# Linear attention with RMS norm and a two-layer MLP: the first pair's v through SyncE and a cast, another order of loads, and stage two rearranged

## The chip, the cores and the metric

The kernel runs on one core of one Trainium2 chip. The core has TensorE (PE; its weight loads are shown apart as PEld), VectorE (DVE), ScalarE (ACT), GpSimd (POOL) and SyncE (SP), and 16 DMA engines, which all queues share. SP, ACT and POOL can issue transfers; in this kernel nearly all loads are issued by POOL, and they turn fp32 in DRAM into fp16 in SBUF on the way. The metric is the device time of one execution in microseconds; lower is better.

## The reference, cut to what matters

There are 8 batches, 8 heads, 576 tokens and a head dimension of 64. The tokens of all batches together (4608) are the rows of an MLP from 512 through 2048 to 512.

```python
kv  = einsum('bhsd,bhse->bhde', k, v)          # 64 x 64 for each head
out = einsum('bhsd,bhde->bhse', q, kv)
rms = sqrt(mean(out * out, axis=-1) + 1e-6)
x   = (out / rms * g_norm), heads side by side: 4608 x 512
h   = x @ w_in                                  # 4608 x 2048
g   = max(h, 0) + alpha * min(h, 0)
y   = g @ w_out                                 # 4608 x 512
```

## The kernel before

The order of the work on every engine is written out by hand (`manual_schedule`), so each engine executes its instructions in the order in which the program emits them, and waits only for data and for free buffers.

**Tiling.** The MLP is done in nine windows `w` of 512 tokens. For a window, `x` is held transposed (`xts[w]`, 128 features by four chunks by 512 tokens). The first product makes 16 groups `u` (or `g`) of 128 hidden features each, four matmuls of 512 columns a group (L600, or L945 and L631 where a group is done by columns). ACT takes the negative part (L609) and DVE combines it into `gt` (L615). In window 0 the second product is plain, one matmul for each of 4 row tiles and 16 groups (`y_run(a, (g,))`, L643, 64 in all). In the other windows it is done with seven products of half size, in the manner of Strassen and Winograd, from sums of `w_out` (`w_sum`) and sums of `gt` (`s_sum`); its matmuls are L796. They are spread over the 16 units of the loop by lists: `X_AT` and `YZ_AT` hold how many matmuls of each sort go into a unit, `S_ALL` and its sisters into which unit a sum goes.

**Attention.** Heads are worked in four pairs `j`. `step_kv` makes k-transposed times v for a pair (L403 for batch 0, L418 for batch 1), `mask_kv` copies it to SBUF on DVE; `step_t` transposes q on PE (L336) and copies it; `step_ot` multiplies the two (L437) and squares the result on ACT; `ssq_mm` sums the squares (L460) and takes the inverse root on ACT; `norm` writes `x` (L476 or L474). From window 2 on, the same is done by rows: `row_kv` (L1122), `rows_mm` (L499), `rows_sq`, `rows_rs`, `rows_norm`, and SP transposes by DMA, both q on its way to `qt_sb` (`dma_t`, L380) and `x` on its way to `xts` (L585). `ROW_AT[w]` says in which unit of window `w-1` each of these stands.

**The start.** The heads of pair 0 arrive by themselves: q by SP and k by ACT in fp32 (`early_pair`, L97), and `cast0` turns them into fp16 (q on DVE, k on ACT). v of pairs 0 and 1 comes by POOL in one cast transfer (`load0("v", 0, 2)`, L168). Then POOL issues everything else in the order of the lines from 261 on: q, k, v of the other pairs, the identity matrix between them, six pieces of `w_in` (piece 0 in two halves of its four chunks, piece 0 to 3 for two groups each, 4 and 5 for four groups each), eight pieces of `w_out` (two groups each), and batch 1. While the pairs are worked, `keep_warm` puts matmuls on constant data into PE's idle time. The first four groups of window 0 are begun chunk by chunk as `norm` delivers the pairs (`m1_parts(g, c)` for groups 0 and 1).

**Stage two.** After the 16 groups of window 0, a written list (L990 to L1093) mixes the 64 `y_run` matmuls with the attention of window 1 (`step_t(1, j)`, `step_kv(1, j)`, `step_ot`, `ssq_mm`, `norm`), the scaling of `w_in` by `g_norm` (`scale_w_in`) and the sums of `w_out` (`w_sum`). The three last matmuls of row tile 3 go into the loop.

**The loop's loads.** `LOADS` places the loads of batch `w+2` into units of window `w`. A load placed at unit `at > 1` stands behind a `gate`, a one-element copy on POOL that reads `gt` of unit `at - 1`; POOL's queue stands still until that is there. q of batch 3 and later is loaded in four pieces of 128 tokens and a remainder of 64 (`load_q`, `load_rem`).

Of the kernel before, what the change touches and what calls it, by code (L numbers as in the profile page):

```python
# [9 lines left out]
FP32 = mybir.dt.float32  # L10
# [7 lines left out]
def kernel(  # L18
# [83 lines left out]
    early_pair(nc.sync, "q", "wsum2")  # L102
    early_pair(nc.scalar, "k", "wsum4")
# [119 lines left out]
    def load_w_in(i):  # L223
        f0, f1 = IN_CUTS[i], IN_CUTS[i + 1]
        t = w_p.tile([P, NC, f1 - f0], FP16, name=f"w_in_sb{i}")
        src = moe_w_in[:, f0:f1].rearrange("(c p) f -> p c f", p=P)
        for c in range(0, NC, NC // 2 if i == 0 else NC):
            n = NC // 2 if i == 0 else NC
            nc.gpsimd.dma_start(out=t[:, c : c + n, :], in_=src[:, c : c + n, :])
        w_in_sb.append(t)  # L230
# [707 lines left out]
    keep_warm(1)  # L938
    norm(0, 1)
    step_kv(0, 3)  # L940
# [9 lines left out]
    first = [ps_h.tile([P, W], FP32, name="h_ps", tag="h1")]  # L950
    first += [ps_o.tile([P, W], FP32, name="h_ps", tag="o") for g in range(2)]
    ssq_mm(0, 2, h_at(0))
    for g in range(2):
        m1_parts(g, 0)
# [34 lines left out]

    y_run(0, (0,))  # L990
    y_run(2, (0,))
# [23 lines left out]
    y_run(0, (4,))  # L1015
    y_run(1, (4,))
    y_run(2, (4,))
    scale_w_in(4, 3, 4, nc.scalar)
    scale_w_in(4, 1, 4, nc.scalar)
    scale_w_in(1)  # L1020
    scale_w_in(3)
    y_run(3, (6,))
    scale_w_in(2)
    y_run(2, (5,))
    step_t(1, 2, S_POOL)
    y_run(1, (7,))
# [3 lines left out]
    y_run(2, (7,))  # L1030
    y_run(3, (5,))
    step_kv(1, 0, O_POOL)
    for nm in ("k", "q"):
        nc.vector.memset(bufs[0][nm][REM:P, TPP, :, :], 0.0)
    y_run(0, (7,))
    step_kv(1, 1, S_POOL)
    y_run(1, (5,))
    y_run(3, (7,))
# [4 lines left out]
    ssq_mm(1, 0, S_POOL)  # L1043
    y_run(0, (8,))
    y_run(1, (8,))
    y_run(3, (8,))
    ssq_mm(1, 1, Q_POOL)
    y_run(0, (6,))
    y_run(0, (9,))
    norm(1, 0)  # L1050
    y_run(3, (9,))
# [3 lines left out]
    w_sum(2, 0)  # L1055
    w_sum(3, 1)
    y_run(2, (8,))
    y_run(2, (9,))
    y_run(2, (11,))
    y_run(1, (11,))  # L1060
    y_run(1, (9,))
    ssq_mm(1, 2)
    y_run(2, (10,))
    y_run(2, (13,))
    y_run(1, (10,))
    w_sum(4, 0)
    step_ot(1, 3)
    y_run(0, (11,))
    y_run(0, (12,))
    y_run(0, (10,))  # L1070
    y_run(0, (13,))
    norm(1, 2)
    w_sum(2, 1)
    y_run(2, (12,))
# [3 lines left out]
    norm(1, 3)  # L1078
    y_run(1, (12,))
# [3 lines left out]
    y_run(2, (14,))  # L1083
    y_out(ys[2], 0, 2)
    y_run(0, (15,))
    y_run(1, (15,))
# [4 lines left out]
    step_t_rem(1, Q_POOL)  # L1091
# [23 lines left out]
    def row_kv(bs):  # L1115
# [26 lines left out]
        5, 6, 8, 9), 'rs': (5, 5, 9, 12), 'norm': (5, 6, 9, 12), 'red': (0, 0, 0, 1)}}  # L1142
# [166 lines left out]
```

## Time and profile before

| | us |
|---|---|
| median of 3 runs | 275.2 |
| lowest and highest run | 273.97, 275.27 |
| profiled execution, its own time | 273.96 |
| its span, first to last instruction | 272.1 |
| PE busy | 264.8 |
| DVE busy | 217.1 |
| ACT busy | 156.5 |
| POOL busy | 86.7 |

The times of all transfers and instructions below are on the span's clock. A line of the timeline gives start, duration, engine, source line, operation, tiles, shapes and count, and in brackets how long the engine was idle before it and what ended that. Ends of matmuls are modelled, and matmuls overlap: a matmul of 512 columns is shown with 379 ns, but the next one starts 216 ns after it, so work on PE is counted here by the distance of starts. A line of the chain gives start, length and what it was; the chain is followed back from the last instruction.

### The profile page before, as it was taken

The numbers are of one execution on the slowest core, as the hardware profiler recorded it, in microseconds if no ns is written. First come the engines' busy times: TensorE is split into PE (matmuls) and PEld (weight loads), VectorE is DVE, ScalarE is ACT, GpSimd is POOL, SyncE is SP. The second block draws the span as 40 slices with busy tenths as digits, with TensorE's granted clock in tenths as the row PEclk, the third lists the DMA queues.
The fourth block names the chain that finished last, engine by engine and source line by source line (L and its number), as shares of the span: only waits on it lengthen the run. The fifth ranks groups of instructions, "written<-read, shape, count | busy, mean of one in ns | idle before, by whom it ended". The sixth has DMA issues, their size and how long they took to land.

```text
span 272.1 us, 6163 instructions
## 1 busy us (share of the span) xinstructions
PE 264.8 (97%) x2286; PEld 168.6 (62%) x2286; DVE 217.1 (80%) x413; ACT 156.5 (58%) x532; POOL 86.7 (32%) x130
## 2 busy tenths in 40 slices
PE   7799999999999999999999999999999999999995
PEld 2354444456766676667666666666667666666684
DVE  7359657999958986998699869986998889878963
ACT  3468575785578447754776467546855864433410
POOL 8773462506431644164415431430110011101100
PEclk9999999999999999999999999999999999999999
DMA  7999999998999999969996999693051122211123
GB/s 149 194 201 203 195 198 193 183 212 95 163 159 197 149 166 125 182 110 172 142 149 117 162 142 149 130 168 77 19 137 40 41 55 81 59 39 40 40 77 119
DMA packets 91570, 35.58 MB, mean 131 GB/s; under 512 B 62980, under 2 KB 89748, under 8 KB 91540
## 3 DMA queue, kind: packets, MB, share of 16 engines
q0 software_dynamic: 57872, 23.83, 71.9%
q1 hardware_dynamic: 32628, 10.34, 23.9%
q10 hardware_dynamic: 1040, 1.02, 1.2%
q8 instruction: 18, 0.29, 0.4%
q14 instruction: 12, 0.10, 0.2%
HBM read 36.71 MB, written 9.44 MB: 170 GB/s over the span
## 4 chain that ended last, share of the span: by engine, by line
PE 83%; DMA 13%; POOL 1%; issue 1%; SPq 1%; ACT 0%; DVE 0%; POOLq 0%
PE h_ps L600 38%; PE yY L796 14%; PE yX L796 10%; PE yZ L796 10%; DMA w_out_sb<-in_moe_w_out_dram 5%; PE y L643 4%; DMA w_in_sb<-in_moe_w_in_dram 3%; DMA qst<-in_q_dram 3%; PE h_ps L631 2%; DMA qt_sb<-qst 2%; PE kv_ps L1122 2%; PE or_ps L499 1%; PE yZ L791 1%; SPq L380 1%; PE kv_ps L418 0%
## 5 line engine op out<-in xcount | busy, mean ns | idle before, releaser
L600 PE MATMUL h_ps<-xt,w_in_sb 128*128 128x512 f16 x540 | 136.2, 379 | 0.0
L609 ACT ACTIVATE m_sb<-h_ps 128x512 f32<-128x512 f32 x144 | 86.5, 601 | 80.3 <-PE h_ps L600 61.5
L615 DVE SCALAR_TENSOR_TENSOR gt<-m_sb,beta_sb,h_ps 128x512 f16<-128x512 f32 x144 | 106.2, 743 | 22.0 <-ACT m_sb L609 18.8
L600 PEld LDWEIGHTS <-w_in_sb 128*128 128x128 f16 x540 | 51.4, 98 | 39.4 <-issue 0.2
L655 POOL DMA_DIRECT2D out_dram<-y_sb x32 | 20.5, 644 | 122.0 <-DVE y_sb L838 57.5
L796 PEld LDWEIGHTS <-s 128*128 128x128 f16 x496 | 48.3, 98 | 11.3 <-DVE s L733 0.3
L796 PEld LDWEIGHTS <-gt 128*128 128x128 f16 x384 | 37.5, 98 | 23.2 <-issue 0.2
L796 PE MATMUL yX<-w_out_sb,gt 128*128 128x256 f16 x256 | 44.6, 273 | 0.0
L796 PE MATMUL yY<-wsum,s 128*128 128x256 f16 x256 | 35.2, 273 | 0.0
L562 ACT ACTIVATE sq_sb<-or_ps 128x64 f16<-128x64 f32 x144 | 30.5, 250 | 2.6 <-PE or_ps L499 2.6
L562 ACT ACTIVATION_READ_ACCUMULATOR sq_sb<-or_ps 128x1 f32 x144 | 30.0, 236 | 0.0
L580 DVE TENSOR_TENSOR x_rows<-or_ps,rstd_r 128x512 f16<-128x512 f32 x27 | 18.4, 686 | 1.0 <-ACT rstd_r L572 1.0
L828 DVE TENSOR_TENSOR u<-yY,p 128x512 f32<-128x512 f32 x16 | 11.0, 689 | 9.6 <-PE yY L796 9.6
L185 POOL DMA_DIRECT2D qst<-in_q_dram x20 | 17.7, 904 | 0.1
L796 PE MATMUL yY<-wsum,gt 128*128 128x256 f16 x128 | 17.6, 273 | 0.0
L796 PE MATMUL yZ<-wsum,s 128*128 128x256 f16 x120 | 17.5, 273 | 0.0
L796 PE MATMUL yZ<-w_out_sb,s 128*128 128x256 f16 x120 | 16.7, 273 | 0.0
L643 PE MATMUL y<-w_out_sb,gt 128*128 128x512 f16 x64 | 16.3, 379 | 0.1
L731 DVE TENSOR_TENSOR s<-gt 128x512 f16<-128x512 f16 x32 | 13.3, 419 | 0.1
L733 DVE TENSOR_TENSOR s<-s,gt 128x512 f16<-128x512 f16 x32 | 12.8, 420 | 0.4
L737 DVE TENSOR_TENSOR s<-gt,s 128x512 f16<-128x512 f16 x32 | 12.7, 418 | 0.0
L735 DVE TENSOR_TENSOR s<-gt 128x512 f16<-128x512 f16 x32 | 12.4, 419 | 0.0
(107 smaller groups left out, 231.1 us busy)
## 6 DMA issues: line engine op xcount, KB each, us to landing
out_dram<-y_sb POOLq DMA_DIRECT2D x16, 256.0 KB, 2.8
kst<-in_k_dram POOLq DMA_DIRECT2D x7, 512.0 KB, 9.9
vst<-in_v_dram POOLq DMA_DIRECT2D x6, 512.0 KB, 8.1
qst<-in_q_dram POOLq DMA_DIRECT2D x20, 128.0 KB, 4.6
w_out_sb<-in_moe_w_out_dram POOLq DMA_DIRECT2D x8, 256.0 KB, 11.0
out_dram<-y_sb SPq DMA_DIRECT2D x5, 256.0 KB, 2.2
w_in_sb<-in_moe_w_in_dram POOLq DMA_DIRECT2D x2, 512.0 KB, 10.0
qst<-in_q_dram POOLq DMA_DIRECT2D x2, 512.0 KB, 12.0
```

The costliest lines, as they stand in the source:

```text
L185: nc.gpsimd.dma_start(out=st[:, t, :, :], in_=srcs["q"][b, :, t * P : (t + 1) * P, :].rearrange("h p d -> p h d"),)
L562: nc.scalar.activation(out=sq[:, half, j], in_=o_ps[:, half, j], func=AF.Square, accum_out=ssq[:, half, j : j + 1],)
L580: nc.vector.tensor_tensor(out=xr[:].rearrange("p j h d -> p h j d"), in0=o_ps, in1=rstd[:].unsqueeze(3).to_broadcast([P, 2, NPAIR, D]), op ...
L600: nc.tensor.matmul(out=h_ps[:], lhsT=w_in_blk(c, g), rhs=xts[w][:, c, :], start=(c == 0), stop=(c == NC - 1),)
L609: nc.scalar.activation(out=neg[w, g][:], in_=h_ps[:], func=AF.Relu, scale=-1.0)
L615: nc.vector.scalar_tensor_tensor(out=gts[w, i][:, r, :], in0=neg.pop((w, g))[:], scalar=beta_sb[:, g : g + 1], in1=h_ps[:], op0=ALU.mult, ...
L643: nc.tensor.matmul(out=y[:], lhsT=gt_cols(w, g, a * P, (a + 1) * P), rhs=w_out_blk(g), start=(n == 1), stop=(n == NF),)
L655: engs[store_turn[0] % len(engs)].dma_start(out=dst, in_=src)
L731: nc.vector.tensor_add(out=t[:], in0=a21, in1=a22)
L733: nc.vector.tensor_sub(out=t[:], in0=sums[w, 1, k][:], in1=a11)
L737: nc.vector.tensor_sub(out=t[:], in0=a12, in1=sums[w, 2, k][:])
L796: nc.tensor.matmul(out=bank, lhsT=lhs, rhs=rhs, start=fresh, stop=(c == NK - 1), skip_group_check=True,)
```

## The change

1. v of pair 0 is loaded in fp32 by SP, as its second transfer, ahead of alpha and `g_norm`; ACT casts it into the fp16 tile behind the cast of k. POOL loads v of pair 1 alone, behind k of pair 1, and the identity is made after the transfer of q for pairs 2 and 3.
2. `w_in`'s piece 0 comes in three transfers instead of two: one chunk, one chunk, two chunks. The first stands between the last k and the last v. `w_out`'s first piece moves from behind `w_in` to the place after piece 1, and the remainder of batch 1's k to the place before the last piece of `w_in`.
3. The `keep_warm(1)` before pair 3's kv goes, and chunk 0 of group 1 takes its place.
4. Stage two's list is in another order; the two first transposes of q and `w_sum(1, 1)` come earlier, and some PSUM banks differ.
5. In the loop: some products and sums go to other units; window 2's inverse root and norm of tiles 0 and 2 come up to one unit later; window 3's rows of tiles 3 and 2 come one unit later, window 8's one unit earlier; k's load goes from unit 1 to unit 3 (now behind a gate) for windows from 2 on; q's remainder is loaded after q's four pieces.

```diff
     early_pair(nc.sync, "q", "wsum2")
+    early_pair(nc.sync, "v", "wsum1")
     early_pair(nc.scalar, "k", "wsum4")
...
-    def load_w_in(i):
+    def load_w_in(i, cs=(0, NC)):
...
+        nc.gpsimd.dma_start(out=w_in_sb[i][:, slice(*cs), :], in_=src[:, slice(*cs), :])
...
-    load0("v", 0, 2)
     load0("q", 1)
     load0("k", 1)
+    load0("v", 1)
+    load0("q", 2, 2)
     ident = const_p.tile([P, P], FP32, name="ident")
     make_identity(nc, ident[:])
-    load0("q", 2, 2)
     load0("k", 2)
     load0("v", 2)
     load0("k", 3)
+    load_w_in(0, (0, 1))
     load0("v", 3)
-    load_w_in(0)
+    load_w_in(0, (1, 2))
+    load_w_in(0, (2, 4))
     load_w_in(1)
+    load_w_out(0)
     load_w_in(2)
     load_w_in(3)
     load_w_in(4)
+    load_rem(1, "k")
     load_w_in(5)
-    load_w_out(0)
     load_main(1, "k")
     load_w_out(1)
-    load_rem(1, "k")
     load_main(1, "q")
...
-    X_AT = [0, 0, 0, 4, 1, 1, 1, 3, 1, 3, 2, 0, 2, 2, 1, 7, 2, 2]
+    X_AT = [0, 0, 0, 4, 1, 2, 1, 2, 0, 4, 2, 0, 2, 2, 1, 7, 2, 2]
...
-    YZ_AT = [3, 7, 6, 5, 5, 6, 7, 4, 5, 7, 5, 4, 5, 6, 5, 0]
-    YZ_1 = [0, 8, 8, 5, 7, 4, 7, 5, 4, 6, 4, 6, 6, 5, 5, 0]
+    YZ_AT = [3, 7, 6, 5, 5, 6, 7, 4, 5, 7, 5, 4, 5, 7, 4, 0]
+    YZ_1 = [0, 9, 7, 5, 7, 4, 7, 4, 5, 6, 4, 6, 6, 5, 5, 0]
...
     cast0("k", nc.scalar.copy)
+    nc.scalar.copy(
+        out=stages[0, "v", 0][0:P0, 0:2].rearrange("p h t d -> p h (t d)"), in_=st32["v"][0:P0]
+    )
...
     step_ot(0, 2, (ps_y, "y"))
-    keep_warm(1)
     norm(0, 1)
-    step_kv(0, 3)
...
+    m1_parts(1, 0)
+    step_kv(0, 3)
     ssq_mm(0, 2, h_at(0))
-    for g in range(2):
-        m1_parts(g, 0)
+    m1_parts(0, 0)
     step_ot(0, 3, Q_POOL, 2)
...
     y_run(0, (2,))
+    w_sum(1, 1)
+    y_run(1, (3,))
+    step_t(1, 0, S_POOL)
+    step_t(1, 1, Q_POOL)
     y_run(2, (3,))
+    y_run(0, (3,))
     scale_w_in(4, 0, 4, nc.scalar)
     y_run(1, (0,))
-    w_sum(1, 1)
-    y_run(1, (3,))
-    y_run(0, (3,))
-    step_t(1, 0, S_POOL)
-    step_t(1, 1, Q_POOL)
     step_t(1, 3, O_POOL)
     y_run(3, (4,))
-    y_run(0, (5,))
+    step_t(1, 2, S_POOL)
     y_run(0, (4,))
...
-    step_t_rem(1, Q_POOL)
+    step_t_rem(1, S_POOL)
...
-        7, 8), 'rs': (3, 9, 10, 9), 'norm': (4, 9, 13, 9), 'red': (1, 1, 0, 1)}, 3: {'kv': 0, 'mm':
-        {4: ((1, 0), (3, 2))}, 'sq': (4, 4, 5, 6, 8, 8, 8, 9), 'rs': (6, 6, 10, 11), 'norm': (6, 7,
-        10, 11), 'red': (0, 0, 1, 0)}, 8: {'kv': 99, 'mm': {1: ((1, 0), (3, 2))}, 'sq': (1, 2, 3, 4,
+        7, 8), 'rs': (3, 9, 11, 9), 'norm': (5, 9, 14, 9), 'red': (1, 1, 0, 1)}, 3: {'kv': 0, 'mm':
+        {4: ((1, 0),), 5: ((3, 2),)}, 'sq': (4, 4, 5, 6, 8, 8, 8, 9), 'rs': (6, 6, 10, 11), 'norm':
+        (6, 7, 10, 11), 'red': (0, 0, 1, 0)}, 8: {'kv': 99, 'mm': {0: ((1, 0), (3, 2))}, 'sq': (1,
...
-        q, k, v = (11, 1, 1) if w == 1 else (12, 1, 5)
+        q, k, v = (11, 1, 1) if w == 1 else (12, 3, 5)
...
                 elif what == "q":
+                    load_q(x[0])
                     load_rem(x[0], "q")
-                    load_q(x[0])
```

More of the change, by code (lines that the diff above doesn't have):

```diff
@@ L221 @@
     IN_CUTS = [i * FW // 2 for i in range(4)] + [i * FW for i in range(2, WQ + 1)]
-    def load_w_in(i):
+    def load_w_in(i, cs=(0, NC)):
         f0, f1 = IN_CUTS[i], IN_CUTS[i + 1]
-        t = w_p.tile([P, NC, f1 - f0], FP16, name=f"w_in_sb{i}")
+        if cs[0] == 0:
+            w_in_sb.append(w_p.tile([P, NC, f1 - f0], FP16, name=f"w_in_sb{i}"))
         src = moe_w_in[:, f0:f1].rearrange("(c p) f -> p c f", p=P)
[L227 to L230, printed above, removed]
+        nc.gpsimd.dma_start(out=w_in_sb[i][:, slice(*cs), :], in_=src[:, slice(*cs), :])
     def scale_w_in(i, h=0, n=1, eng=None):
@@ L948, in m1_parts @@
             )
-    first = [ps_h.tile([P, W], FP32, name="h_ps", tag="h1")]
-    first += [ps_o.tile([P, W], FP32, name="h_ps", tag="o") for g in range(2)]
+    first = [
+        ps_h.tile([P, W], FP32, name="h_ps", tag="h1"),
+        ps_o.tile([P, W], FP32, name="h_ps", tag="o"),
+        ps_o.tile([P, W], FP32, name="h_ps", tag="o"),
+    ]
+    m1_parts(1, 0)
+    step_kv(0, 3)
     ssq_mm(0, 2, h_at(0))
-    for g in range(2):
-        m1_parts(g, 0)
+    m1_parts(0, 0)
     step_ot(0, 3, Q_POOL, 2)
@@ L988, in y_run @@
             y_mm(ys[a], 0, a, g)
+    y_run(2, (0,))
     y_run(0, (0,))
-    y_run(2, (0,))
     y_run(3, (1,))
@@ L1003 @@
     y_run(0, (2,))
+    w_sum(1, 1)
+    y_run(1, (3,))
+    step_t(1, 0, S_POOL)
+    step_t(1, 1, Q_POOL)
     y_run(2, (3,))
+    y_run(0, (3,))
     scale_w_in(4, 0, 4, nc.scalar)
     y_run(1, (0,))
-    w_sum(1, 1)
-    y_run(1, (3,))
-    y_run(0, (3,))
-    step_t(1, 0, S_POOL)
-    step_t(1, 1, Q_POOL)
     step_t(1, 3, O_POOL)
     y_run(3, (4,))
-    y_run(0, (5,))
+    step_t(1, 2, S_POOL)
     y_run(0, (4,))
     y_run(1, (4,))
+    y_run(0, (5,))
     y_run(2, (4,))
     scale_w_in(4, 3, 4, nc.scalar)
-    scale_w_in(4, 1, 4, nc.scalar)
[L1020 to L1026, printed above, removed]
+    scale_w_in(2)
+    scale_w_in(1)
+    y_run(3, (5,))
+    y_run(2, (5,))
+    scale_w_in(3)
+    y_run(2, (7,))
+    y_run(3, (6,))
+    scale_w_in(4, 1, 4, nc.scalar)
     y_run(2, (6,))
@@ L1029 @@
     scale_w_in(4, 2, 4, nc.scalar)
-    y_run(2, (7,))
-    y_run(3, (5,))
+    y_run(1, (7,))
     step_kv(1, 0, O_POOL)
@@ L1034 @@
         nc.vector.memset(bufs[0][nm][REM:P, TPP, :, :], 0.0)
+    y_run(3, (7,))
+    step_kv(1, 1, O_POOL)
     y_run(0, (7,))
-    step_kv(1, 1, S_POOL)
     y_run(1, (5,))
-    y_run(3, (7,))
     step_ot(1, 0)
@@ L1043 @@
     ssq_mm(1, 0, S_POOL)
+    y_run(1, (8,))
     y_run(0, (8,))
-    y_run(1, (8,))
-    y_run(3, (8,))
-    ssq_mm(1, 1, Q_POOL)
     y_run(0, (6,))
@@ L1050 @@
     norm(1, 0)
+    y_run(3, (8,))
+    ssq_mm(1, 1, Q_POOL)
+    w_sum(2, 0)
     y_run(3, (9,))
@@ L1054 @@
     step_ot(1, 2)
-    w_sum(2, 0)
+    y_run(1, (11,))
     w_sum(3, 1)
     y_run(2, (8,))
+    y_run(1, (10,))
+    w_sum(4, 0)
     y_run(2, (9,))
     y_run(2, (11,))
-    y_run(1, (11,))
-    y_run(1, (9,))
     ssq_mm(1, 2)
-    y_run(2, (10,))
     y_run(2, (13,))
-    y_run(1, (10,))
-    w_sum(4, 0)
     step_ot(1, 3)
@@ L1069 @@
     y_run(0, (12,))
+    y_run(2, (10,))
+    y_run(1, (9,))
     y_run(0, (10,))
@@ L1072 @@
     norm(1, 2)
-    w_sum(2, 1)
-    y_run(2, (12,))
     y_run(3, (12,))
@@ L1078 @@
     norm(1, 3)
+    y_run(2, (12,))
+    y_run(2, (14,))
+    w_sum(2, 1)
     y_run(1, (12,))
@@ L1082 @@
     y_run(2, (15,))
-    y_run(2, (14,))
     y_out(ys[2], 0, 2)
+    y_run(1, (15,))
     y_run(0, (15,))
-    y_run(1, (15,))
     y_out(ys[0], 0, 0)
@@ L1138 @@
     ROW_AT = {2: {'kv': 5, 'mm': {0: ((0,),), 7: ((1, 3),), 8: ((2,),)}, 'sq': (1, 1, 7, 7, 8, 10,
[3 rows of a table removed]
-        5, 6, 8, 9), 'rs': (5, 5, 9, 12), 'norm': (5, 6, 9, 12), 'red': (0, 0, 0, 1)}}
[3 rows of a table added]
+        2, 3, 4, 5, 6, 8, 9), 'rs': (5, 5, 9, 12), 'norm': (5, 6, 9, 12), 'red': (0, 0, 0, 1)}}
     for w in range(4, B):
```

10 lines of the change are left out of this document (5 added, 5 removed).

## The prediction

> **What bounds the kernel now.** I read the page's busy shares, then the chain that ended last in order of time, then the timeline wherever that chain leaves TensorE (PE).
>
> ```profile
> PE 264.8 (97%) x2286; PEld 168.6 (62%) x2286; DVE 217.1 (80%) x413; ACT 156.5 (58%) x532; POOL 86.7 (32%) x130
> ```
>
> The chain (start, length, what), up to 34 us and around its one later transfer:
>
> ```profile
> 3.97 6.83 DMA qst<-in_q_dram
> 11.82 7.30 DMA w_in_sb<-in_moe_w_in_dram
> 19.40 14.39 DMA w_out_sb<-in_moe_w_out_dram
> 33.84 1.82 PE y L643 x7
> ...
> 72.05 5.59 DMA qt_sb<-qst
> 77.77 0.41 PE or_ps L499 x16
> 78.18 0.97 PE h_ps L600 x4
> ```
>
> PE is busy for 97% of the span, and the chain goes through transfers only up to 33.84 us and once more, from 72.05 to 77.64. The rest is PE. So only these two places can give time back; a new PE wait elsewhere costs its whole length. The timeline of those places:
>
> ```profile
> 7.88 0.38 PE L403 MATMUL kv_ps<-vst,ksb 96*64 96x64 f16 x12 [0.84 <-DMA vst<-in_v_dram]
> 12.36 0.38 PE L403 MATMUL kv_ps<-vst,kst 96*64 96x64 f16 x12 [0.37 <-DMA vst<-in_v_dram]
> 13.59 0.38 PE L297 MATMUL warm_ps<-y_sb 128*128 128x512 f16 x1
> 14.44 0.38 PE L460 MATMUL ssq_ps<-sq_sb,mask 128*128 128x512 f16 x1 [0.16 <-ACT sq_sb L444]
> 32.88 0.70 PEld L336 LDWEIGHTS <-qst 128*64 128x64 f16 x24 [0.42 <-DMA qst<-in_q_dram]
> 33.84 1.82 PE L643 MATMUL y<-w_out_sb,gt 128*128 128x512 f16 x7
> 35.12 0.69 DVE L705 TENSOR_TENSOR wsum<-w_out_sb 128x1024 f16<-128x1024 f16 x1 [3.15 <-DMA w_out_sb<-in_moe_w_out_dram]
> 37.11 0.20 PEld L418 LDWEIGHTS <-kst 128*64 128x64 f16 x8 [0.42 <-DMA vst<-in_v_dram]
> 77.77 0.41 PE L499 MATMUL or_ps<-kv_masked,qt_sb 64*128 64x64 f16 x16 [0.48 <-DMA qt_sb<-qst]
> ```
>
> PE waits for v's pairs at 7.88 and 12.36, for q, w_out and v of batch 1 at 32.9 to 37.1, and for a transposed tile of q at 77.77. The windows view (PE, PEld, DVE, ACT, POOL busy; clock, DMA share, GB/s) shows the transfers saturated meanwhile:
>
> ```profile
> 14.20:29.30 15.10, 14.90 (x83) 7.62 (x78) 11.86 (x19) 10.96 (x21) 7.34 (x10) 1.00 1.37 200
> 29.30:38.80 9.50, 9.40 (x86) 4.43 (x85) 5.74 (x13) 5.35 (x10) 5.27 (x7) 1.00 1.40 199
> ```
>
> Landings below are issue plus time to landing of single transfers: v2 12.22, v3 13.76, w_in pieces 14.42 and 15.06 (halves of the first), 16.40, 17.79, 19.12, 21.61, 24.16; w_out0 25.50, k(1) 28.13, w_out1 29.37, k(1)'s remainder 29.83, q(1) 32.53, w_out2 33.79, w_out3 35.02, v(1) halves 36.86 and 38.57.
>
> **The start, part by part.** v0 leaves POOL's first transfer (0.84 us of issue) for SP, issued second at about 1.15 (the row of q: 0.40 each); alpha and g_norm move back 0.40. A pair of heads takes 0.73 us of transfer (k2 11.52 to v2 12.22 to k3 12.96). q and k land at 5.23 and 5.59, so v0 in fp32 lands about 6.4 (0.73 later plus a little for q1 beside it). ScalarE's cast costs what k's does, 0.83 (L898), is queued behind it (ends 6.44) and ends about 7.3; ACT was idle there until 9.07, so it delays nothing. First kv: 7.88 to about 7.4.
>
> That is not yet a gain. kv(0,2) waits for v2 until 12.36 although PE was free at 11.99, so the chain can move only as far as v2's landing moves. The bytes ahead of v2 are the same (q and k of pairs 0 to 2, q3, three pairs of v). What may change is the ramp: in the packets from 3.5 to 4.5 us I count 281 KB read (fp32; fp16 written counts double) against some 372 KB a microsecond from 5.0 on, and v0 can fill this: 91 KB, 0.25 us. From below: nothing, or a loss of 0.3 if three queues disturb q and k; from above 0.48, the whole move of the first kv. I take s = 0.2, nearest the counted hole.
>
> make_identity goes behind q2-3 on POOL: 0.6 us later, ready about 4.6; the cast that reads it is at 4.76 behind DVE's memsets. Covered; without the memsets 0.6 on the first transpose, still under v2's wait.
>
> The warm matmul goes (0.22 us) and m1_parts(1,0) fills its place. It needs w_in's first quarter, 0.32 (half of 15.06-14.42=0.64) behind k3: 13.28-s. v3 comes 0.32 later, 14.08-s, so kv(0,3) moves from 13.90 to 14.1-s. The mask after it waited for norm(0,1) until 14.51 on DVE anyway, and the squares of pair 3 wait for ACT's rstd of pair 2 until 15.51. So the saved 0.22 becomes a wider wait at ssq(0,3): gain s, no more.
>
> **Stage one pays.** w_out0 (25.50-24.16=1.34) now lies ahead of w_in2: w_in2 at 19.13-s, w_in4 at 22.95-s, w_in5 (behind k's remainder, 0.46) at 25.95-s. PE reaches group 4 at 18.97-s: waits 0.16; group 8 at 22.59-s: waits 0.36; group 12 at 26.41-s: nothing. Behind these waits stand PE's whole queue and the groups' ACT and DVE reads, which have no other work then. POOL issues one transfer more (0.7); each issue waits for the landing of the eighth before it (8.12 after v's 7.84), and the last w_in was issued at 13.29 for 24.16, so POOL's issue stays covered. Stage two starts at 29.85-s instead of 29.33.
>
> **Stage two takes that back.** Before: 28 y matmuls (0.216 each, 6.05) and four step_t (about 0.25 each) up to kv(1,0) at 37.12, with waits of 0.31 for w_out2 and 0.15 for w_out3 and 0.1 for q. After: thirteen y's end at 32.66-s, q has landed at 32.53-s; w_out2 and w_out3 land before their first reader, and kv(1,0) starts at about 37.2 to 37.3-s (0.1 for one more change between transposes and y's), v's half being there at 36.86-s. The waits are gone because PE comes later, not because it did less. kv(1,2) has v at 38.57-s against PE at 38.9-s. DVE's w_sum(1,1) waits for w_out3 as before (3.15 us row), with only the scalings behind it, and mask follows at 37.5 as before; ACT's copies of step_t and scalings only change places in a queue that idled 2.54 there. From there PE had no wait worth 0.2 up to 47.7; norm(1,3) now has nine y's behind it instead of eight. Start in all: -0.2 + 0.1 = **-0.1** (bounds -0.9 and +0.5: with both gains of s and the waits 0.46; with s = 0 and nothing taken back).
>
> **The loop.** Window 2 waits at 77.77 for the third transposed piece of q(3), issued by SP at 72.05 after q's piece landed at 72.00, and 5.6 us under way. q's four pieces now come before the remainder: 0.70 (its issue, L198) to 0.8 earlier. Its readers, rows tiles 3 and 2, move from unit 4 to unit 5, one unit (28/16 = 1.75 us) later. Both cover the wait of 0.48 to 0.67 (the profile's idle and the start-to-start gap). I take **-0.6**; the remainder is the last tile read, so its 0.7 lies beside a unit that does not need it. Next late: tile 1's two pieces, landed by 73.24, 3.5 us of cover. k's load waits now for a gate at unit 3, two units later; behind that gate are POOL's stores and v, which waited for their own gates to 77.96. k is read a window later, 20 us of cover. X_AT, YZ_AT, S lists: the same products and sums in other units, on a PE with no wait there; 0, but the ninth product of YZ_1 at unit 1 needs the sum that DVE ended near 71.2, and PE would reach it at 71.35: +0.1 at worst. norm of tile 2 at unit 14: ends near 67.55 against PE's 67.67: 0 to +0.1. Rows of window 8 a unit earlier, step_t_rem in another bank: 0.
>
> **Sum**: -0.1 - 0.6 = -0.7. Against the profiled execution, 273.96 (span 272.1 and 1.86 around it): 273.3. That run was the lowest level; the median is 275.2, so I forecast 274.5. Half a per cent is 1.4 us, and the three runs alone spread over 1.3.
>
> **Rivals.** (a) The start gains in full: s = 0.48, waits of 0.46 saved and 0.67 in the loop: -1.6, 273.6. For it: the hole in the ramp; against: v2, w_in2 and w_in4 decide. (b) The move does not do what it says: stage one's 0.52 is not taken back, or window 2 waits again at unit 5: 275.1. For: transfers of 5.6 us there; against: 1.75 us of cover. (c) Slower: ACT's cast waits until pair 1's v, written to the same tile, has landed (9.3): kv(0,0) at 10.1, +2.3 at the first kv, +1.9 at kv(0,2), +1.5 at kv(1,0), -0.6 in the loop: 276.1. It decides if the cast starts after 9.3. Against: kv(0,2) read its half of vst at 12.36 while v3 landed in the other at 13.76. (d) Slower: k's load, 3.5 us later, meets the transposes of x. One took 7.3 us beside k and v (82.99) and 3.8 beside nothing (89.35 to 93.15), reader at 95.81. With 7.3 it lands at 96.65: 0.84 a window, four windows, 3.4: 277.9. It decides if k and v land after 92 (v now at 90.15). Against: the same bytes end at the same time.
> (e) Clock: the first ten warm matmuls stand 0.43 apart, later ones 0.216; if PE's idle time at the start put it back to 0.43, the some 16 matmuls from 14.4 on would lose 0.216 each: +3.4, 277.9 with the loop's gain. Against: the longest wait there is under 1 us. The Trainium skill (TensorE: Matmul & The Clock Gate, Part 1) says that the clock falls to half after an idle window of about 3.4 us; by that rule, too, no wait here is long enough.
> (f) alpha becomes the start's wait: it landed at 5.87, 0.64 after q on the same queue. Behind v0 that is 7.0; its transpose (0.13) and two warm matmuls (0.43) precede kv(0,0) on PE, which then starts at 7.6. v2 still decides: no time, so it sits inside the forecast. The Trainium skill (DMA: Bandwidth & Descriptors, Queues, rings and completion order) has each engine take one queue's descriptors in ring order, which speaks against putting v ahead of alpha.
>
> **Numbers.** Forecast 0.54, (a) 0.15, (b) 0.10, (c) 0.06, (d) 0.08, (e) 0.02, others, taken as slower, 0.05. The forecast's own range is 273.3 to 275.2: the runs' lower level puts a quarter of it under 273.8. Faster: 0.13+0.13+0.01=0.27; slower: 0.07 of (d), 0.02 of (c), 0.08 of the rest, 0.17; same 0.56. Range: low 272.8 (lowest run 273.97 less 1.2), high 276.2 (holds (c), leaves out (d), (e)).
>
> **What will show it.** First kv near 7.4 with a cast before it; kv(0,2) at 12.2 or so; waits before groups 4 and 8; stage two from 29.6 on with no wait for w_out2; or_ps of window 2 with no wait. Wrong if kv(0,0) is later than 7.88, if kv(1,2) moves by over 0.5, or if L631 or L499 wait for transposes in any window.

## The result and the profile after

The changed kernel takes 275.6 us (median of 22 runs, 274.56 to 277.69) against 274.4 for the kernel before (22 runs on the same chips): a ratio of 1.0054, 95% interval 1.0039 to 1.0070, by that ratio some 1.5 us slower. The forecast was 274.5 against 275.2, no change or a small gain. The profiled execution of the changed kernel took 276.31 with a span of 274.4, 2.3 more than the span of before, and 0.7 over its own median.

The page's busy line of the changed kernel. PE is still busy for 97%: 1.3 of the 2.3 more in the span count as busy, part of it work at the half speed told of below.

```profile
PE 266.1 (97%) x2285; PEld 168.1 (61%) x2285; DVE 217.2 (79%) x413; ACT 157.1 (57%) x533; POOL 88.2 (32%) x135
```

The chain that ended last, in order of time (start, length, what), its four transfers:

```profile
2.54 5.29 DMA y_sb<-in_g_norm_dram
...
52.96 7.12 DMA qt_sb<-qsb
...
65.43 5.22 DMA xt<-x_rows
...
231.94 4.53 DMA xt<-x_rows
```

No load of q, `w_in` or `w_out` is left in it. Instead it begins with `g_norm`, 256 bytes, and passes through three transposes by DMA, the last of them for window 8. The timeline at these places (start, us, engine, line, what, and the idle time before with its releaser):

```profile
6.83 0.83 ACT L909 CAST vst<-v 96x768 f16<-96x768 f32 x1 [0.33 <-DMA v<-in_v_dram]
7.97 0.20 PE L914 MATMUL alpha_ps<-ident,y_sb 17*128 17x17 f32 x1 [1.56 <-DMA y_sb<-in_g_norm_dram]
8.94 0.53 PE L404 MATMUL kv_ps<-vst,ksb 96*64 96x64 f16 x12
12.08 0.38 PE L404 MATMUL kv_ps<-vst,kst 96*64 96x64 f16 x12
60.12 0.40 PE L513 MATMUL oc_ps<-qt_sb,kv_masked 128*128 128x128 f16 x4 [0.39 <-DMA qt_sb<-qsb]
70.69 0.38 PE L632 MATMUL h_ps<-xt,w_in_sb 128*128 128x128 f16 x4 [0.51 <-DMA xt<-x_rows]
79.14 0.52 PE L500 MATMUL or_ps<-kv_masked,qt_sb 64*128 64x64 f16 x24
```

Two things that the change was made for can be seen: v is cast at 6.83, and the reader of q in window 2 (79.14) no longer waits. But PE stands for 1.56 us before alpha's transpose, and two readers wait that did not before. The windows view of two stretches behind that first wait (us, then PE, PEld, DVE, ACT, POOL busy; granted clock, DMA share, GB/s):

```profile
4.86:8.27 3.41, 1.34 (x17) 0.66 (x16) 1.21 (x4) 1.66 (x2) 2.88 (x5) 1.00 1.26 206
8.27:11.69 3.42, 3.42 (x30) 1.26 (x29) 0.60 (x4) 0.60 (x1) 2.75 (x5) 0.50 1.31 199
```

For 3.41 us PE is granted half its clock, so that kv(0,0) to kv(0,1) takes 3.14 instead of 2.36. From profile to profile, window 1 starts 1.13 later (48.85 against 47.72), window 1 takes 0.57 more, window 2 0.22 more, windows 3 to 7 the same to 0.01, and the stretch from window 8 to the end 0.42 more, 0.28 of it before the last tile of `x` of window 8: 2.34 together. This split is that of two executions; two profiles of the kernel before differ by 1.1 (0.47 in the start, 0.64 in window 2).

### The profile page after: what moved, and what is told of

Its sections match the earlier page's. It is cut to its first block, busy times and chain, and to the rows that moved or that the text cites. A ratio compares the mean times of both kernels' runs of the same rounds, so it can differ in the third digit from the quotient of the medians.

```text
span 274.4 us, 6176 instructions
## 1 busy us (share of the span) xinstructions
PE 266.1 (97%) x2285; PEld 168.1 (61%) x2285; DVE 217.2 (79%) x413; ACT 157.1 (57%) x533; POOL 88.2 (32%) x135
## 4 chain that ended last, share of the span: by engine, by line
PE 85%; DMA 8%; ACT 2%; DVE 2%; SPq 1%; issue 1%
PE h_ps L601 38%; PE yY L797 15%; PE yZ L797 9%; PE yX L797 8%; PE y L644 5%; DMA xt<-x_rows 4%; DMA qt_sb<-qsb 3%; DMA y_sb<-in_g_norm_dram 2%; PE h_ps L632 2%; PE or_ps L500 1%; PE kv_ps L1128 1%; SPq L381 1%; PE ssq_ps L461 1%; PE warm_ps L298 1%; DVE x_rows L581 1%
## 5 line engine op out<-in xcount | busy, mean ns | idle before, releaser
L797 PE MATMUL yX<-w_out_sb,gt 128*128 128x256 f16 x256 | 43.6, 273 | 0.0
```

Source lines behind the costliest of these rows:

```text
L797: nc.tensor.matmul(out=bank, lhsT=lhs, rhs=rhs, start=fresh, stop=(c == NK - 1), skip_group_check=True,)
```

## The experiments

The starts, for all kernels run. "Window 1, 2" and "end" are the lengths from the start of a window to the next, the last from the start of window 8 to the end; the ratio is against the kernel before on the same chip, with its 95% interval. The control (before again) came out 0.17% from 1, and most intervals reach a quarter of a per cent to either side. So the times tell versions with the old start (e6, f4, f3) from the changed kernel, but none of the repairs below: from 1.0029 to 1.0067, their intervals overlap that of the changed kernel. What each part costs is therefore read from the profiles, one execution each.

| run | kv(0,0) | stage two | kv(1,0) | window 1 starts | window 1 | window 2 | end | ratio |
|---|---|---|---|---|---|---|---|---|
| before | 7.88 | 29.33 | 37.12 | 47.72 | 19.95 | 28.14 | 38.98 | 1 |
| before again | 7.40 | 28.87 | 36.65 | 47.25 | 19.95 | 27.50 | 39.01 | 1.0017 (0.9993-1.0041) |
| after | 8.94 | 30.62 | 38.33 | 48.85 | 20.52 | 28.36 | 39.40 | 1.0054 (1.0039-1.0070) |
| e3 v alone | 8.77 | 31.36 | 38.85 | 49.45 | 20.78 | 28.42 | 39.62 | 1.0054 (1.0025-1.0082) |
| e8 v, alpha on ACT | 8.04 | 30.03 | 37.52 | 48.12 | 20.50 | 27.49 | 40.00 | 1.0048 (1.0018-1.0079) |
| e2 wait filled | 8.84 | 29.75 | 37.46 | 47.98 | 21.05 | 28.34 | 39.17 | 1.0029 (1.0007-1.0052) |
| e1 alpha on ACT | 7.72 | 29.66 | 37.37 | 47.89 | 20.82 | 27.70 | 39.71 | 1.0060 (1.0039-1.0082) |
| e7 no v | 7.63 | 30.65 | 38.36 | 48.88 | 21.32 | 27.70 | 38.67 | 1.0067 (1.0045-1.0090) |
| f1 no v, old loads | 7.37 | 29.24 | 37.92 | 48.45 | 21.80 | 27.70 | 38.83 | 1.0050 (1.0024-1.0076) |
| f2 alpha on ACT, old loads | 7.62 | 28.53 | 36.82 | 47.34 | 20.29 | 27.70 | 39.77 | 1.0043 (1.0018-1.0069) |
| h2 old stage two | 8.24 | 29.88 | 37.36 | 47.96 | 20.26 | 27.70 | 39.29 | 1.0035 (1.0009-1.0061) |
| h1 sum back | 8.18 | 30.20 | 37.91 | 48.43 | 20.26 | 28.25 | 39.38 | 1.0051 (1.0024-1.0077) |
| e5 alpha on ACT, late k(3) | 7.68 | 29.72 | 37.44 | 47.96 | 19.94 | 27.70 | 39.93 | 1.0039 (1.0017-1.0060) |
| h3 v on ACT, mended | 7.55 | 28.59 | 37.29 | 47.82 | 20.27 | 27.70 | 39.99 | 1.0061 (1.0042-1.0080) |
| e4 old loop | 8.55 | 30.55 | 38.26 | 48.78 | 20.38 | 28.23 | 39.59 | 1.0106 (1.0074-1.0138) |
| e6 loop alone | 7.46 | 28.94 | 36.73 | 47.33 | 19.95 | 28.50 | 38.70 | 1.0007 (0.9982-1.0031) |
| f4 loop, q at 12 | 7.41 | 29.17 | 36.93 | 47.53 | 19.95 | 29.44 | 38.87 | 1.0002 (0.9979-1.0025) |
| f3 one more transfer | 7.59 | 29.13 | 36.79 | 47.39 | 19.95 | 27.57 | 39.43 | 0.9979 (0.9954-1.0004) |

### The start: v ahead of alpha

**e3_v_alone**: the kernel before with the v part alone.

```diff
     early_pair(nc.sync, "q", "wsum2")
+    early_pair(nc.sync, "v", "wsum1")
...
-    load0("v", 0, 2)
     load0("q", 1)
     load0("k", 1)
+    load0("v", 1)
+    load0("q", 2, 2)
...
     cast0("k", nc.scalar.copy)
+    nc.scalar.copy(
```

> The kernel before with the v part alone: v of pair 0 by SP ahead of alpha, ACT's cast, POOL's order q1, k1, v1, q2-3, identity. Theory: the same wait of 1.6 us for g_norm, the same half clock, kv(0,0) at 8.9 instead of 7.88, kv(0,2) near 13.6, stage two 1.2 later than before (30.5), of which its waits of 0.46 for w_out come back: 0.8 slower than the kernel before. My forecast's view (v's early start is worth nothing or a little, no loss): same as before or 0.2 faster.

**e8_v_alpha_act**: the same, with alpha and `g_norm` issued by ACT, ahead of its table load (the table load's move is left out here).

```diff
-    nc.sync.dma_start(out=alpha_row[0:NF, 0:P], in_=moe_alpha[:].rearrange("(g p) -> g p", p=P))
+    nc.scalar.dma_start(out=alpha_row[0:NF, 0:P], in_=moe_alpha[:].rearrange("(g p) -> g p", p=P))
...
-        nc.sync.dma_start(
+        nc.scalar.dma_start(
```

> The kernel before with the v part alone, and alpha and g_norm issued by ACT ahead of its table load. Theory (the v part's cost is that g_norm waits behind v): the 1.5 us which the v part alone lost come back: within 0.3 of the kernel before, kv(0,0) at 7.7, no half clock. Rival (a load in fp32 or the cast is the cost in itself): still 1 us or more above the kernel before.

**e1_alpha_act**: the changed kernel with this last edit.

> The changed kernel, but alpha and the two g_norm transfers are issued by ACT, behind k and ahead of the table load, instead of by SP behind v. Theory (the wait for g_norm behind v, with the half clock after it, is what moves the start): alpha's transpose back from 7.97 to about 6.4 us, no half clock between 8.27 and 11.69, first kv about 7.7 instead of 8.94, kv(0,2) about 12.1 instead of 13.67. Not all of it reaches stage two: w_in2 and w_in4 landed at 19.53 and 23.29, and eight groups of 0.866 follow the latter, so stage two can start no earlier than 30.2 (30.62 in the changed kernel): 0.4 us faster than the changed kernel. Rival (the start costs nothing in the end, the loop's new waits do): first kv moves, time of the whole within 0.2 of the changed kernel.

**e2_fill_wait**: the changed kernel with eight warm matmuls in the wait; the wait itself stays.

```diff
     step_t(0, 0, h_at(0))
+    keep_warm(8)
     alpha_ps = ps_y.tile([P, NF + 1], FP32, name="alpha_ps", tag="y")
```

> The changed kernel with eight more warm matmuls (1.7 us at 0.216) ahead of alpha's transpose, in PE's idle time from 6.3 to 7.97. Separates the wait from the clock that falls after it. Theory that the half clock is the larger part: alpha's transpose stays at 8.0, first kv at 8.5 (8.94), but kv(0,2) at 12.6 (13.67) as the 4.1 us of chain between them run at full clock; stage two from 30.2 (w_in4), so 0.4 us faster, like the run with alpha on ACT. If the wait alone is the cost: first kv 8.8 or later and kv(0,2) within 0.3 of 13.67, time unchanged. If the warm matmuls do not hold the clock: the half clock shows again after 8 us.

The v part alone costs as much as the whole change (1.0054). Its timeline at alpha's transpose and further on, and that of the run with the wait filled:

```profile
7.61 0.26 PE L914 MATMUL alpha_ps<-ident,y_sb 17*128 17x17 f32 x1 [1.08 <-DMA y_sb<-in_g_norm_dram]
...
13.17 0.61 PE L438 MATMUL ot_ps<-qt_sb,kv_masked 128*128 128x512 f16 x1
```

```profile
6.31 1.90 PE L298 MATMUL warm_ps<-y_sb 128*128 128x512 f16 x8
8.14 0.23 PE L915 MATMUL alpha_ps<-ident,y_sb 17*128 17x17 f32 x1
```

The profile of e3 is no typical one: PE is at half speed from the start up to 14.06. A matmul of 512 columns is shown with 0.61 as late as 13.17 (0.39 at full speed), though the windows view prints a clock of 1.00 there. Its own time, 277.44, is 2.3 above the median of its runs, so its late stage two (31.36) does not stand for them.

With the wait filled alpha comes as late as ever (8.14) and kv(0,0) at 8.84, there is no half clock, and stage two starts 0.87 earlier than in the changed kernel (29.75 against 30.62). Not all of this is the clock: `w_in`'s fifth piece landed at 22.68 in e2 and at 23.29 in the changed kernel, where eight groups of 0.866 behind it end at 30.2 at best. So the half clock cost 0.4 there, and up to 0.9 where `w_in` comes earlier. Taking the wait down to 0.5 (e1) moves kv(0,0) by 1.1 and stage two only by 0.09 more, to 29.66, because there it waits for `w_in`:

```profile
18.93 3.63 PE L601 MATMUL h_ps<-xt,w_in_sb 128*128 128x512 f16 x16 [0.50 <-DMA w_in_sb<-in_moe_w_in_dram]
22.74 0.61 PE L601 MATMUL h_ps<-xt,w_in_sb 128*128 128x512 f16 x2 [0.18 <-DMA w_in_sb<-in_moe_w_in_dram]
```

So alpha and the clock explain the start of the changed kernel, but a start without them meets the next limit. On ACT, with the kernel before around it (e8), alpha waits for 1.19 all the same, and half clock follows from 8.88 to 12.30: the bytes of v ahead delay `g_norm` on another queue too. h3, below, has this the other way round, v on ACT's queue and `g_norm` on SP's, issued when it was before; its wait is 0.73, and the transpose comes at 6.85 instead of 6.29. The ratio of e1 fell short of what its profile saved; its end is 0.31 longer than that of the changed kernel and its window 1 0.30.

### The order of loads and stage two

**e7_no_v**: the changed kernel without the v part (v of pairs 0 and 1 by POOL as before). **f1_no_v_old_loads**: this, with two loads back in their places:

```diff
     load_w_in(1)
-    load_w_out(0)
     load_w_in(2)
     load_w_in(3)
     load_w_in(4)
-    load_rem(1, "k")
     load_w_in(5)
+    load_w_out(0)
     load_main(1, "k")
     load_w_out(1)
+    load_rem(1, "k")
```

**f2_act_old_loads**: e1 with these two loads back.

> The changed kernel without the v part (v of pairs 0 and 1 by POOL in one transfer and first, as before); pieces of w_in, stage two and loop as changed. If the v part is what makes the changed kernel slower: 1.2 to 1.5 below it, thus within 0.3 of the kernel before, kv(0,0) near 7.9, no half clock, waits of 0.2 and 0.4 before groups 4 and 8. If the rearranged loads and stage two are the cost: still 1 to 1.5 above the kernel before.

> The changed kernel without v of pair 0 by SP and its cast, and with w_out's first piece and the remainder of batch 1's k back at their old places in the order of loads. Theory (the load order, with w_out0 ahead of w_in2 to w_in5, made stage one 1.2 late in the run without v): no wait before groups 4, 8 and 12, stage two starts at 29.2 to 29.6 instead of 30.65, window 1 starts at 47.6 to 47.9, and the ratio falls from 1.0067 to about 1.002. Rival (the split of w_in's first piece, or the new stage two, costs the time): stage two still starts after 30.2, or window 1 starts more than 18.4 after stage two; ratio 1.005 or more.

> The changed kernel with alpha and g_norm issued by ScalarE, and the same two loads back at their old places: only the start of the experiment with alpha on ScalarE is left, without its waits for w_in. Theory: kv(0,0) at about 7.7, waits before groups 4 and 8 (0.66 and 0.34) gone, stage two at 28.7 to 28.9; but stage two then waits for w_out2, w_out3 and q again (0.3 to 0.6 in all), window 1 at 47.0 to 47.5; ratio 1.002 to 1.004, since the waits of window 1 and the longer tail are left. Rival (the start is not limited by these loads): stage two at 29.5 or later, ratio 1.006 as with alpha on ScalarE alone.

Without v, and with no wait for alpha, the changed kernel is as slow as with it (1.0067). Its largest wait at the start is for `w_in`'s fifth piece, as the idle time of the weight loads shows (PE itself loses 0.94 there, by the distance of starts):

```profile
23.73 6.59 PEld L600 LDWEIGHTS <-w_in_sb 128*128 128x128 f16 x32 [1.26 <-DMA w_in_sb<-in_moe_w_in_dram]
```

With the two loads back stage two starts 1.41 earlier (29.24 against 30.65), and 1.13 earlier in f2 than in e1 (28.53 against 29.66): the two loads ahead of `w_in` did that. But kv(1,0) gains only 0.44 and the ratio is 1.005, not the 1.002 expected. The new list of stage two calls for q after 13 matmuls instead of 16, and now q is not there:

```profile
33.11 0.64 PE L336 MATMUL qt_ps<-ident,qst 128*64 128x128 f16 x16 [0.90 <-DMA qst<-in_q_dram]
...
61.00 0.40 PE L512 MATMUL oc_ps<-qt_sb,kv_masked 128*128 128x128 f16 x4 [1.67 <-DMA qt_sb<-qsb]
```

f2 says it most plainly: stage two starts at 28.53, 0.8 before the kernel before and 0.34 before its control, and kv(1,0) at 36.82, no earlier than in that control (36.65). The transposes of q wait for 0.51 at 32.01. What ends the start is the landing of q, `w_out` and v of batch 1, behind some 200 GB/s from 5 us on; with this list a faster stage one has nothing to give. A faster stage one with the old list was not run. In the control that list already gives 0.3 to waits for w_out2 and w_out3, and v lands at 36.38, 0.27 before kv(1,0), so there is little left to gain; this is argued, not shown.

**h2_old_stage_two**: the changed kernel with the list of stage two as before.

> The changed kernel with the whole list of stage two as it was before. Theory: from the start of stage two (30.6, or with alpha's wait as drawn 30.4 to 30.9) to kv(1,0) it takes 7.6 to 7.9, no less with the new list (7.71) than with the old, since PE comes after w_out2 and w_out3 either way; the first transposed piece is issued 0.97 after window 1 starts, no wait above 0.2 before oc_ps, window 1 at 19.95 to 20.15; ratio 1.002 to 1.004. Rival (the new list does take something back): kv(1,0) 8.1 or more after stage two starts, ratio 1.006 or more.

With the old list it takes 7.48 from stage two's start to kv(1,0) and 18.08 to window 1; the same two figures, 7.49 and 18.09, come out of e3 and e8, which have that list too and start as late. With the new list it is 7.71 or 7.72 and 18.23 or 18.24 (after, e1, e2, e4, e5). The new list has the same 28 matmuls of `y` and four transposes ahead of kv(1,0), but enters the transposes three times instead of twice; on the way in the first transpose starts 0.31 after the last `y` (0.216 from one `y` to the next), on the way out the next `y` starts 0.15 after the last transpose. In the kernel before the way to window 1 is 18.39, in its control 18.38. So PE's waits there are worth 0.3, and the new list takes half of that for itself.

### Window 1: the sum ahead of q's copy

**h1_sum_back**: the changed kernel with one line back in its place.

```diff
     norm(1, 2)
+    w_sum(2, 1)
     y_run(3, (12,))
...
     y_run(2, (14,))
-    w_sum(2, 1)
     y_run(1, (12,))
```

**e5_act_late_k3**: e1 with k and v of batch 3 loaded at units 4 and 6 of window 1 instead of 1.

```diff
-        q, k, v = (11, 1, 1) if w == 1 else (12, 3, 5)
+        q, k, v = (11, 4, 6) if w == 1 else (12, 3, 5)
```

> The changed kernel with one line moved: the sum w_sum(2, 1) stands behind norm(1, 2) again, as before, instead of behind norm(1, 3). Theory: with it VectorE's copy of q of batch 2 (the row 49.54, 0.69 long, which stood 2.17 behind window 1's last norm of batch 1 started, against 1.20 before) comes 0.5 to 0.7 earlier, SyncE's first transposed piece is issued 0.9 to 1.0 after window 1 starts instead of 1.47, the third ahead of k(3)'s load or with it; the wait of 0.56 before oc_ps falls to 0 to 0.2, window 1 takes 19.95 to 20.15 instead of 20.52, ratio 1.002 to 1.004. Rival (the later start itself, or transfers of batch 1 still under way, delay these pieces): the wait stays at 0.4 or more, ratio 1.005.

> The changed kernel with alpha and g_norm issued by ACT, and k and v of batch 3 loaded at units 4 and 6 of window 1 instead of both at unit 1. Theory: the third transposed piece of q(2), issued 0.5 us after the k load (52.01 against 51.52 in the run with alpha on ACT) and landing with it (59.42, 59.47), holds PE at oc_ps for 0.86. With k out of its way it lands near 55.7, the wait is gone, and the time is 0.6 to 0.9 below the run with alpha on ACT (275.43): about 274.7. Rival (the wait moves to the transposes of x before window 2): wait at L632 instead, time unchanged.

DVE's rows between the last norm and q's copy, and the issues that follow, first of the kernel before, then after, then with the sum back:

```profile
46.69 0.69 DVE L474 TENSOR_TENSOR xt<-ot_ps,rstd 128x512 f16<-128x512 f32 x1 [0.34 <-ACT rstd L464]
...
47.89 0.69 DVE L209 COPY qsb<-qst 128x2048 f16<-128x2048 f16 x1
...
48.68 4.10 SPq L380 DMA_TRANSPOSE qt_sb<-qsb  x3
...
51.40 0.91 POOL L176 DMA_DIRECT2D kst<-in_k_dram  x1
```

```profile
47.61 0.69 DVE L475 TENSOR_TENSOR xt<-ot_ps,rstd 128x512 f16<-128x512 f32 x1 [1.48 <-ACT rstd L465]
48.22 0.68 DVE L710 TENSOR_TENSOR wsum<-w_out_sb,wsum 128x1024 f16<-128x1024 f16 x1
48.93 0.69 DVE L714 TENSOR_TENSOR wsum<-w_out_sb,wsum 128x1024 f16<-128x1024 f16 x1
49.54 0.69 DVE L210 COPY qsb<-qst 128x2048 f16<-128x2048 f16 x1
```

```profile
48.40 0.68 DVE L210 COPY qsb<-qst 128x2048 f16<-128x2048 f16 x1
49.18 3.90 SPq L381 DMA_TRANSPOSE qt_sb<-qsb  x3
```

The sum stands between the norm and the copy of q (the copy starts 1.93 behind the norm, 1.20 before; the 2.17 of the expectation is not in these rows) and makes SP's three transposed pieces 0.5 later against window 1. In the kernel before the third is issued at 51.51, beside k(3)'s load (51.40), and lands at 57.18; in the changed kernel 0.48 behind it (52.96 against 52.48), and lands with it, at 60.08 and 60.05. The same pairing is in e1 (59.42, 59.47), e2 (59.74, 59.82) and e7 (60.92, 61.00). With the sum back the third piece is issued at 51.82 with k(3) at 51.86, lands at 58.03, and the wait is gone; with k(3) later (e5) it lands 3.3 after its issue, and window 1 takes 19.94. The Trainium skill (DMA: Bandwidth & Descriptors, Queues, rings and completion order) says that a transfer's completion mark on a DMA engine is written only after all earlier writes of that engine, of other queues too; landing together with a load of 512 KB agrees with it. No run here tells this from the two transfers simply sharing the engines. In h1 0.27 of the gain went into a wait on `gt` at 54.16; the same 0.27 stands in h2 and h3 (53.69, 53.55), the other runs with the sum back beside the new loop, and its cause is open. The ratio of h1 (1.0051) does not show the rest.

### The loop

**e6_loop_alone**: the kernel before with the loop part (the lists, `ROW_AT`, the order of `load_q` and `load_rem`, k at unit 3). **e4_old_loop**: the changed kernel without it. **f4_loop_q12**: e6 with q of batch 3 one unit later.

```diff
-        q, k, v = (11, 1, 1) if w == 1 else (12, 3, 5)
+        q, k, v = (12, 1, 1) if w == 1 else (12, 3, 5)
```

> The kernel before with the loop's part alone (lists, ROW_AT, unit of k's load, q's remainder last). My forecast's term: 0.6 faster than before, no wait at or_ps of window 2. By the difference of the run with the old loop and the changed kernel: 1.4 faster. If new waits at oc_ps or at the last columns of window 2 belong to the loop's part: same or slower.

> The changed kernel with the loop's part undone: X_AT, YZ_AT, YZ_1, the S lists, ROW_AT, the unit of k's load and the order of q's remainder as before. Start, loads up to batch 1 and stage two as changed. My forecast's term (the loop's part is worth 0.6, the wait of 0.48 to 0.67 at L500 in window 2): 0.6 slower than the changed kernel, with a wait near 79. Rival (the loop's part costs: the new waits of 0.39 before oc_ps at 60.12 and 0.51 before the last columns of window 2 at 70.69 come from it): 0.5 to 1 faster. If these waits come from the start's shift and not from the loop's part, they stay here, and the time is within 0.3 or 0.6 slower.

> The kernel before with the loop part of the change (as in the run of that part alone) and q of batch 3 loaded at unit 12 of window 1 instead of 11, 1.7 us later. Theory (the 0.81 wait for tile 3 of x at 68.74 came because q's pieces now run in its 5 us under way): the transpose of tile 3 lands before 67.5 and the wait goes; the third transposed piece of q lands near 75.7, before its reader at 77.8, so that wait does not come back; window 2 takes 27.7 instead of 28.14 (before) and 28.50 (loop part alone), 0.4 to 0.6 faster than before, ratio 0.997 to 0.9985. Rival (transposes simply take 5 to 7 us there): the wait moves on to or_ps at 77 to 80, window 2 at 28.2 or more, ratio 1.000.

**h4_before_again**: the kernel before, nothing changed.

> The kernel before, unchanged, as a control. Every theory expects a ratio of 1.000 with an interval of about 0.0025 to either side. Theory (the wait of 0.48 for the transposed q in window 2 is one execution's): window 2 takes anything from 27.57 to 28.5, and the wait stands before another reader, or nowhere. Rival (it is fixed by the order of the loads): a wait of 0.4 to 0.7 before or_ps at 77 to 78, as in the profile shown.

The last tile of `x` of window 2 in e6 and in f4, and the reader of q in the control:

```profile
68.74 0.38 PE L631 MATMUL h_ps<-xt,w_in_sb 128*128 128x128 f16 x4 [0.64 <-DMA xt<-x_rows]
...
77.18 0.53 PE L499 MATMUL or_ps<-kv_masked,qt_sb 64*128 64x64 f16 x24
```

```profile
69.81 0.38 PE L631 MATMUL h_ps<-xt,w_in_sb 128*128 128x128 f16 x4 [1.51 <-DMA xt<-x_rows]
```

```profile
76.30 0.76 PE L499 MATMUL or_ps<-kv_masked,qt_sb 64*128 64x64 f16 x40
```

The loop part alone is worth nothing (1.0007). It removes the wait for q, and tile 3 of `x` waits instead. Whether q's pieces running beside it are the reason, f4 does not settle. There the wait doubled, but v(3) landed at 63.31 against 61.71 in e6, the first transposed tile of `x` at 65.10 against 62.93, and SP issued tile 3's transpose 0.76 later, at 64.44: q's first piece, moved to 64.39, still ran beside it. And the control has no wait in window 2 at all: all 40 matmuls in one row, window 2 in 27.50. Of six profiles with the old loop, three have a wait for q (28.14 to 28.42) and three none (27.49 to 27.57); of those with the new loop, seven take 27.70 and five 28.25 to 29.44. Undisturbed the new loop is 0.2 slower. The e4 ratio, 1.0106, stays unexplained: its profile shows no more than the waits of the table and a span of 274.3, and its own time, 276.06, is the lowest of its six runs.

### The end, and v through ScalarE

**f3_one_more**: the kernel before with one tiny transfer more on SP.

```diff
+    more_sb = const_p.tile([1, D], FP32, name="more_sb")
+    nc.sync.dma_start(out=more_sb[:], in_=g_norm[:].unsqueeze(0))
```

**h3_v_act_mended**: the changed kernel with v issued by ACT behind k, the two loads back, and the sum back.

```diff
     early_pair(nc.sync, "q", "wsum2")
-    early_pair(nc.sync, "v", "wsum1")
     early_pair(nc.scalar, "k", "wsum4")
+    early_pair(nc.scalar, "v", "wsum1")
```

> The kernel before with one more transfer on SP: g_norm (256 bytes) a third time, into a tile that nobody reads, behind the second. Nothing reads it; the transfers behind it get the next semaphores. Theory (the order of the semaphores decides how long the end takes): starts of all windows as before within 0.1, the time from the last landing to the end 1.3 to 1.6 instead of 0.9 to 1.2, ratio 1.0005 to 1.0015. Rival (the end's spread is chance, or comes from v's transfer itself): the end as before, ratio 1.000.

> The changed kernel with v of pair 0 issued by ScalarE behind k instead of by SyncE (alpha and g_norm keep their places on SyncE), w_out's first piece and k's remainder at their old places, and w_sum(2, 1) behind norm(1, 2). Theory: alpha lands at 5.9 to 6.0, nothing waits for it; kv(0,0) at 7.6 to 7.9, stage two at 28.5 to 28.8, but kv(1,0) still at 36.8 to 37.2 because q, w_out2 and v land when they did; window 1 19.95 to 20.1, window 2 27.7 to 28.3; ratio 0.999 to 1.002, and with the end at 39.7 instead of 39.0, if that comes from transfers added to ScalarE's queue, at the upper end of it. Rival (v and its cast cost by themselves, by the queue they take): kv(0,0) after 8.3, ratio 1.004 or more.

The end goes with the transfers at the start: 38.67 to 39.01 in the six profiles without a transfer more, 39.17 to 39.62 in the seven with one more on SP (0.18 to 0.28 of it, in four, before the last tile of `x` of window 8), 39.71 to 40.00 in the five with more on ACT. SP's last act is to go through the semaphores of its stores in a fixed order, some 0.06 each; with one transfer more the last store has another semaphore, and in f3 1.63 pass from the last landing to the end, against 1.20 in the kernel before. The semaphore alone does not set this: with the same last one it is 1.35 in the changed kernel and 1.63 in f3, 1.20 in the kernel before and 0.92 in e6. But the time of f3 is 0.9979 of before (0.9954 to 1.0004), so the timed runs do not bear out the half microsecond of the profiles; why the last store lands later after transfers on ACT is open.

h3 is the start that the change was thought to give: kv(0,0) at 7.55, stage two at 28.59. Nothing is left of it at kv(1,0), 37.29, behind a wait of 0.92 for q at 32.48, and the ratio is 1.0061, not the 0.999 to 1.002 expected. Against the control its profile is 2.06 longer: 0.57 up to window 1, 0.32 in window 1, 0.20 in window 2 and 0.98 at the end. No version beat the kernel before.

## Why the prediction was wrong

**"v2 still decides: no time" (rival f).** This is the step that failed first. The sizes on the way were nearly right: v landed at 6.80 (6.4 predicted), the cast ended at 7.66 (7.3), alpha landed at 7.03 (7.0), POOL's v of pair 2 0.6 earlier. But the same transpose reads `g_norm` as well, whose two transfers stand behind alpha on SP's queue, and for them I had only the 0.40 of the issue and no landing. The last one released the transpose, at 7.97 instead of about 7.0 (6.29 before). kv(0,0) came at 8.94 and not at 7.6, and kv(0,2), at 13.67, stood behind kv(0,1) and not behind v2, which had landed at 11.63.

**Rival (e), the clock, at 0.02.** That "the longest wait there is under 1 us" holds only without a new wait for `g_norm`. The wait was 1.56 and the clock fell, earlier than (e) had it (from 8.27, not 14.4) and for less than its 3.4: by e2 0.4 to 0.9 at stage two. The rule of the Trainium skill that I cited there, an idle window of about 3.4 us (TensorE: Matmul & The Clock Gate, Part 1), did not protect: the window of 4.86 to 8.27 held 1.34 of work.

**"Stage one pays", 0.52.** The time is right where the start is free: predicted 29.65 for stage two, 29.66 in e1, with both waits at the places named (0.50 and 0.18 idle, 0.16 and 0.36 predicted). The price of the two loads is not: it is 1.13 (e1 against f2) and 1.41 (e7 against f1), because without them stage two could start before 29.33, at 28.53 in f2.

**"Stage two takes that back."** A mis-sized term. I counted waits of 0.31, 0.15 and 0.1; the gaps of 0.15 are the change from transposes to `y`, and stay (0.15 three times in the new list). Waits worth 0.3 went, one change more came: 0.15 back by the start of window 1, not 0.46.

**"The loop. I take -0.6."** The wait was real, but one execution's: the control has none. Its removal is worth up to 0.6 in some executions, nothing in others, and the new loop loses 0.2 undisturbed and waits for `x` elsewhere. All three signs of being wrong that the prediction named came true: kv(0,0) later than 7.88 (8.94), kv(1,2) moved by over 0.5 (38.83 to 39.97), and a wait for transposes in the line that was L631 before (L632, 0.51 at 70.69).

**What had no term.** The copy of q behind `w_sum(2, 1)`, 0.57 in window 1 (0.26 of it back in h1): I had followed DVE's queue to the norms and not to the copy that starts SP's transposes.

**What held.** ACT's cast did not wait for pair 1's v (c), k's later load met no transposes of `x` (d): windows 3 to 7 are the same to 0.01.

The parts do not add: v alone 1.0054, everything but v 1.0067, both 1.0054. By the profiles each delays the same point: stage two starts at 30.62 in the changed kernel, at 30.65 without v, and the later of the two counts.

## What to carry to other kernels

Before a start is made faster, look for what ends it: here q of batch 1 landed between 32.0 and 33.3 in every profile, and the 0.3 to 0.8 us won in stage one (f2, against the control and against before) were a wait in stage two. Here a small transfer behind a large one, on its queue or beside it, was moved by the bytes ahead, so look for the tiny operand whose reader stands first in an engine's queue. A wait for a DMA that one profile shows should be seen in a second execution of the same kernel before a part of the sum is built on it.

## What the runs showed of the hardware

The granted clock changes only at the edges of stretches of 3.413 us, whose position differs from run to run. Counted from the rows of PE (whose ends are modelled), a stretch with 1.25, 1.40, 1.44 or 2.07 us without work (e8, e4, h1, after) was followed by one at half clock; stretches with 1.18 (h3), 1.20 (before) and 1.22 (h2) were not. For h2 and e8, windows view:

```profile
6.17:9.58 3.41, 2.19 (x30) 0.87 (x28) 0.99 (x4) 1.11 (x3) 2.84 (x5) 1.00 1.31 201
9.58:12.99 3.41, 3.25 (x63) 1.76 (x64) 1.70 (x4) 2.33 (x5) 2.87 (x4) 1.00 1.32 191
```

```profile
5.47:8.88 3.41, 2.16 (x31) 0.99 (x30) 1.21 (x5) 1.66 (x2) 3.08 (x6) 1.00 1.30 201
8.88:12.30 3.42, 3.42 (x30) 1.22 (x31) 0.85 (x3) 1.28 (x2) 2.93 (x4) 0.50 1.32 199
```

Almost the same work stands in both first rows, and one run loses its clock. e3 stands apart: there PE did not leave the half speed of the start before 14.06. The Trainium skill (TensorE: Matmul & The Clock Gate, Part 1) has the window's length, 3413 ns, and that it runs free of the kernel, and both agree; that a whole window must be idle does not. The kernel before stood close to this edge with its own 1.20 (0.80 in its control).
